# Small-matmul bursts of a recurrent mixer: one burst for the scores of a pair and one for the outputs of a step, with a wider spacing in the planner

## The chip, the cores and the metric

The kernel runs on one core of one Trainium2 chip. The metric is the device time of one execution in microseconds (us), lower is better. The engines are TensorE (PE in the profile, with its weight loads as PEld), VectorE (DVE), ScalarE (ACT), GpSimd (POOL) and SyncE (SP), which issues the transfers.

## The reference

A gated linear recurrence over 768 positions for 4 batches and 8 heads of 48, and two feed-forward layers on its 3072 rows:

```python
# attention: B, H, S, D = 4, 8, 768, 48
for t in range(S):
    cur = einsum('bhd,bhe->bhde', u * kt, vt)
    y[:, :, t] = einsum('bhd,bhde->bhe', rt, state + cur)
    state = wt[:, :, :, None] * state + einsum('bhd,bhe->bhde', kt, vt)
x = y.transpose(0, 2, 1, 3).reshape(3072, 384)
x = (sigmoid(x @ w_gate) * (x @ w_val)) @ moe_w_out     # 384 -> 1536 -> 384
h = x @ w_in                                            # 384 -> 2048
out = (h * tanh(softplus(h))) @ moe2_w_out              # 2048 -> 384
```

## The kernel before

The sequence is cut into 24 steps of 32 positions (`step(j)`), and two steps make a pair (`NP` = 12 pairs, numbered from 0). For a pair, `fine(p)` builds the products inside blocks of 8 positions on POOL and DVE (tiles `pt` and `blk`, sums in `A`), and `coarse(p)` turns what it needs (tiles `RD`, `KD`, `WD`) and computes the scores between blocks on TensorE (tile `lp`, two PSUM banks, L644). Eight tasks `merge` on ACT or DVE, three copies each, bring the scores from PSUM into the tile `X` (L665): four for the first step of the pair (bank `lp..0`), four for the second. Right behind the scores, one more product rescales 24 of the 56 columns of `RD` (L624, shape 128x768).

A step then has three pieces on TensorE. `rows_out` makes its outputs from `X` and `v` and from the state `s` and `RD` (tile `yp`, two PSUM banks, L742); a split into two half-precision parts follows on ACT and DVE (tile `xs`), and transposes send it to `xt`, the operand of the feed-forward layer. `outer` makes the update of the state (tile `kp`, L841), which DVE adds (`s`, L852). All three are bursts of small float32 matmuls with 32 or 64 rows and 48 columns; the tile program issues 64 of them for the scores of a pair, and the trace records two per matmul.

The feed-forward matmuls are the dense work: `gate` (tile `gv`, L901) and `out1` (tile `o`, L969), in groups of nine 128x128 by 128x256 matmuls. A pair has 24 groups of `gv` and, from the second on, 12 of `o`. While the dense groups of one pair run, the bursts of the next pair are put between them. The decoding of the weights (tiles `wgs`, `wvs`, `wos`, then `wis`, `wps`) is further work of ACT, DVE and POOL, at the beginning and after the last pair.

The three PSUM tiles `lp`, `yp` and `kp` share three banks in turn (`next_at`): the first bank of `kp` in the first step of a pair was the second of the scores, and its second bank was the first of `yp`.

The order of the work on each engine is not written by hand. Each piece is a task with a guessed cost and with the tiles that it reads and writes; `Plan.run` works out how late each may begin, then walks through time and gives each engine the task that is due earliest among those that are ready. A task may name two engines with a cost for each; the one that is free first takes it. Tasks marked `burst` are held back while another task is ready and the last burst ended less than `SPACE` ago:

```python
tired, late, rank, t = min(
    (t.burst and now < rested, t.late, t.rank, t) ...
if t.burst:
    rested = t.end + SPACE
```

Before, scores and outputs are each two tasks of cost `BURST` with the same operands and banks: half of the 8 (or 4) columns each.

Of the kernel before, what the change touches and what calls it, by code (L numbers as in the profile page):

```python
# [7 lines left out]
F32 = mybir.dt.float32  # L8
# [7 lines left out]
B, H, S, D = 4, 8, 768, 48  # L16
# [7 lines left out]
RC = 56  # L24
# [19 lines left out]
SHARED = (0,)  # L44
WHOLE = range(1, 12, 2)
COLD = 1.9
BURST = 0.58
PARTS = ((), (0,), (1,), (2, 3))
SPACE = 1.9
SWEEPS = 1  # L50
ENGS = ("pool", "dve")
W1HI = {"act": 0.83}
# [12 lines left out]
class Plan:  # L65
# [30 lines left out]
    def run(self):  # L96
# [35 lines left out]
        while len(order) < len(self.tasks):  # L132
# [14 lines left out]
            if t.burst:  # L147
                rested = t.end + SPACE
            if e != "none":
# [11 lines left out]
def mixer_moe_kernel(  # L161
# [30 lines left out]
    pp = sa.enter_context(tc.tile_pool(name="pp", bufs=1, space=PS, side="right"))  # L192
# [13 lines left out]
    def attn(eng, cost, fn, reads=(), writes=(), lat=SEM, burst=False):  # L206
        add(eng, cost, fn, [*reads, "attention"], writes, lat, burst)
# [217 lines left out]
    lps = {}  # L425
    late = {}
    yps = {}
# [8 lines left out]
    def next_at():  # L436
        nat[0] += 1
        return ("at", nat[0] % 3)
# [144 lines left out]
    def coarse(p, cells):  # L583

        R, K, W = (("blk", p % 2, i) for i in range(3))
        RD, KD, WD = ("RD", p % 2), "KD", ("WD", p % 2)
        X = [[("X", p % 2, e, n) for n in range(4)] for e in range(2)]
        banks = [next_at() for _ in range(2)]
# [39 lines left out]
                op=ALU.mult,  # L628
            )

        def scores(part):
            if not part:
                for e in range(2):
                    lps[p, e] = pp.tile(
                        [128, 8, RC - 8], F32, tag=f"at{banks[e][1]}", name=f"lp{p}_{e}"
                    )
            for i in range(4 * part, 4 * part + 4):
                for e in range(2):
                    for q in range(2):
                        for g in range(2):  # L640
                            o = 64 * (g ^ e) + 32 * q
                            x = HG * e + 8 * q + i
                            gs = slice(64 * g, 64 * g + 64)
                            nc.tensor.matmul(  # L644
                                lps[p, e][o : o + 32, i],
                                kd[p][gs, x],
                                rd[p][gs, x, 8:],
                                start=True,
                                stop=True,
                            )  # L650
# [21 lines left out]
        attn(both, 0, lambda e: scaled(e, 5, 6, 1, 2), [WD], [(*RD, 2)])  # L672
        attn({"dve": 0.6, "pool": 1.05}, 0, lambda e: scaled(e, 2, 4, 2, 1), [WD, (*RD, 2)], [(*RD, 1)])
        parts = [(*RD, n) for n in range(3)]
        for half in range(2):
            attn("pe", BURST, lambda _, n=half: scores(n), [*parts, KD], banks, burst=True)
        attn("dve", 1.9, flip_a, [*cells], X[0] + X[1])
        for e in range(2):
            for n in range(4):
# [40 lines left out]
    def step(j):  # L720
        p, e = divmod(j, 2)
        V = ("v", j % 3)
        X = [("X", p % 2, e, n) for n in range(4)]
        RD = [("RD", p % 2, n) for n in range(2)]
        S, nxt = ([("s", i % 2, x) for x in range(2)] for i in (j, j + 1))
        ybanks = [next_at() for _ in range(2)]

        def rows_out(part):
            if not part:
                for t in range(2):  # L730
                    yps[j, t] = pp.tile(
                        [128, 512], F32, tag=f"at{ybanks[t][1]}", name=f"yp{j}_{t}"
                    )
            for h in range(2 * part, 2 * part + 2):
                for n in range(2 if j else 1):
                    for t in range(2):
                        for b in range(B):
                            g = b // 2 ^ t
                            gs = slice(64 * g, 64 * g + 64)
                            i = b % 2 * H + 4 * t + h  # L740
                            x = HG * e + i
                            nc.tensor.matmul(  # L742
                                yps[j, t][32 * b : 32 * b + 32, h * D : h * D + D],
                                (rd if n else xp)[p][gs, x, :C],
                                (ss if n else vs)[j][gs, i, :],
                                start=(n == 0),
                                stop=(n == 1 or j == 0),
                            )
# [28 lines left out]
                    out=xt[p][:, i, :, 128 * e : 128 * e + 128], in_=xss[j][:, i]  # L777
                )

        for part in range(2):  # L780
            attn(
                "pe",
                BURST * (COLD if j < 4 else 1.0),
                lambda _, part=part: rows_out(part),
                [*X, *RD, V, *S],
                ybanks,
                burst=True,
            )
        xs = [("xs", j % 2, t) for t in range(2)]
        attn("none", 0, lambda _: new_xs(), [], [(*xs[t], i) for t in range(2) for i in range(2)])  # L790
        for t in range(2):
# [40 lines left out]
        kbanks = [next_at() for _ in range(2)]  # L832
# [31 lines left out]
                )  # L864
        cold = COLD if j < 4 else 1.0
        parts = [("KK", p % 2, g, q, h) for g in range(2) for q in range(2) for h in range(2)]
        attn("pe", 1.08 * cold, outer, [*parts, V], kbanks, burst=True)
        for hf in range(2):
            attn("dve", 0.48, lambda _, hf=hf: join(hf), [kbanks[hf]], [nxt[hf]])
        if j + 3 < NJ:  # L870
# [411 lines left out]
    for i in range(6):  # L1282
        cs = slice(256 * i, 256 * i + 256)
        for name, dst, w in (("wg", wgs, wg), ("wv", wvs, wv)):
            if count in WHOLE:
                load_raw((name, i), lambda: dp, in_cols(w, cs), (KC, 256), count % 3)
                part = lambda dst=dst, cs=cs: dst[:, :, :, cs]
# [11 lines left out]
    def tail1(p):  # L1299
        coarse(p, cells[p])  # L1300
        keys(p)
        step(2 * p)
# [134 lines left out]
```

## Time and profile before

| | us |
|---|---|
| time, median of three runs | 953.5 (953.48 to 955.08) |
| the profiled execution: its own time | 953.2 |
| its span, first to last instruction | 951.1 |
| PE busy | 887.4 (93%) |
| DVE busy | 653.6 (69%) |
| ACT busy | 484.7 (51%) |
| POOL busy | 478.5 (50%) |
| matmuls of `lp`, `yp`, `kp` in the trace | 1536, 3008, 1472 |

The profile is of one execution. A row of the timeline joins equal instructions that follow each other, with the start of the first and the time until the end of the last; ends of matmuls are modelled, so the start of the next row says more about the pace than the end does. What stands in brackets is idle time of the engine ahead of the row and what ended it. [...]

### The profile page before, as it was taken

How to read it: one execution, taken by the hardware profiler on the slowest of the kernel's cores; microseconds unless marked ns; L12 is line 12 of the kernel's file. 1: busy time of each engine (PE TensorE's matmuls, PEld its weight loads, DVE VectorE, ACT ScalarE, POOL GpSimd, SP SyncE). 2: the span in 40 equal slices, each digit the busy share in tenths (PEclk: the TensorE clock that was granted, in tenths of full speed). 3: DMA queues.
4: the chain of work that ended last, by engine and by line, in shares of the span. 5: the costliest groups of instructions: out<-in, count | busy, mean ns of one | idle time of the engine just before them, and what ended most of it. 6: DMA issues, size and time to landing. Idle time of an engine off the chain costs nothing.

```text
span 951.1 us, 29379 instructions
## 1 busy us (share of the span) xinstructions
PE 887.4 (93%) x12808; PEld 707.6 (74%) x12808; DVE 653.6 (69%) x1073; ACT 484.7 (51%) x1086; POOL 478.5 (50%) x528
## 2 busy tenths in 40 slices
PE   0478799999999999999999999999999999999998
PEld 0366478888888888888888886567677676776788
DVE  7999975666775867686678888785565655655541
ACT  2668854333435253433336777675565655556540
POOL 8999922636364546446364265553343434434330
PEclk9988799999999999999999999999999999999999
DMA  9456732222222223222222660010200102000000
GB/s 311 128 167 199 247 104 77 59 74 73 69 58 68 67 65 97 50 77 60 58 57 79 195 207 12 12 40 1 68 1 10 59 2 67 1 18 18 1 34 34
DMA packets 56464, 71.89 MB, mean 76 GB/s; under 512 B 20752, under 2 KB 37648, under 8 KB 56208
## 3 DMA queue, kind: packets, MB, share of 16 engines
q1 hardware_dynamic: 56336, 70.03, 24.9%
q8 instruction: 100, 1.64, 0.7%
q14 instruction: 28, 0.23, 0.1%
HBM read 56.64 MB, written 9.44 MB: 69 GB/s over the span
## 4 chain that ended last, share of the span: by engine, by line
PE 79%; DVE 8%; ACT 5%; POOL 4%; DMA 2%; issue 2%; SPq 0%; ACTq 0%; DVEq 0%; POOLq 0%
PE gv L901 23%; PE h L1079 20%; PE o L1194 17%; PE o L969 12%; ACT X L665 3%; PE yp L742 3%; PE kp L841 2%; DVE X L665 2%; PE lp L644 2%; POOL blk L487 1%; DMA raw_wp<-wo 1%; DVE A L507 1%; POOL sum_wp L333 1%; POOL pt L487 1%; DVE wps L333 1%
## 5 line engine op out<-in xcount | busy, mean ns | idle before, releaser
L1079 PE MATMUL h<-x,wis 128*128 128x512 f16 x864 | 199.9, 379 | 0.0
L487 POOL TENSOR_TENSOR blk<-blk 128x384 f32<-128x384 f32 (+3 forms) x139 | 124.0, 908 | 103.4 <-DMA blk<-rkw 72.0
L901 PE MATMUL gv<-xt,wvs 128*128 128x256 f16 x1296 | 169.1, 277 | 4.7 <-POOL wvs L307 3.7
L901 PE MATMUL gv<-xt,wgs 128*128 128x256 f16 x1296 | 167.2, 275 | 4.8 <-ACT sig L912 1.9
L969 PE MATMUL o<-gt,wos 128*128 128x256 f16 x1296 | 166.4, 274 | 3.7 <-POOL wos L307 2.0
L1113 POOL TENSOR_TENSOR sum<-e 128x256 f32<-128x256 f32 x96 | 71.4, 744 | 183.4 <-ACT e L1090 183.3
L1079 PEld LDWEIGHTS <-wis 128*128 128x128 f16 x864 | 83.5, 98 | 82.9
L901 PEld LDWEIGHTS <-wvs 128*128 128x128 f16 x1296 | 126.2, 99 | 23.4 <-POOL wvs L307 4.3
L969 PEld LDWEIGHTS <-wos 128*128 128x128 f16 x1296 | 126.5, 98 | 22.4 <-POOL wos L307 2.2
L901 PEld LDWEIGHTS <-wgs 128*128 128x128 f16 x1296 | 123.3, 98 | 23.6 <-issue 2.7
L487 POOL TENSOR_TENSOR pt<-blk 128x384 f32<-128x384 f32 x93 | 106.5, 1168 | 44.1 <-DMA blk<-rkw 42.5
L1090 ACT ACTIVATE e<-h 128x512 f32<-128x512 f32 x96 | 57.2, 596 | 84.6 <-PE h L1079 83.7
L929 ACT CAST gt<-gv 128x512 f16<-128x512 f32 x72 | 42.0, 584 | 77.3 <-DVE gv L917 77.1
L665 ACT COPY X<-lp 24x64 f32<-24x64 f32 x180 | 46.1, 256 | 54.8 <-DVE X L665 26.0
L1194 PE MATMUL o<-wps,gt 128*128 128x192 f16 x612 | 74.0, 246 | 0.0
L917 DVE SCALAR_TENSOR_TENSOR gv<-gv,sig 128x512 f32<-128x512 f32 x72 | 50.8, 706 | 33.2 <-ACT sig L912 16.7
L912 ACT ACTIVATE sig<-gv 128x512 f32<-128x512 f32 x72 | 43.2, 599 | 52.8 <-PE gv L901 52.5
L932 DVE TENSOR_TENSOR gt<-gv,gt 128x512 f16<-128x512 f32 x72 | 49.4, 686 | 29.1 <-ACT gt L929 28.6
L1132 DVE SCALAR_TENSOR_TENSOR gt<-e,gt 128x256 f16<-128x256 f32 x41 | 27.5, 683 | 49.6 <-ACT gt L1127 49.6
L1194 PE MATMUL o<-wps,wgs 128*128 128x192 f16 x498 | 59.4, 246 | 0.0
L1194 PE MATMUL o<-wps,wos 128*128 128x192 f16 x456 | 57.1, 246 | 0.0
L1194 PEld LDWEIGHTS <-gt 128*128 128x128 f16 x612 | 52.9, 98 | 3.3
(107 smaller groups left out, 1470.0 us busy)
## 6 DMA issues: line engine op xcount, KB each, us to landing
v<-vt SPq DMA_DIRECT2D x96, 96.0 KB, 3.0
blk<-rkw SPq DMA_DIRECT2D x22, 384.0 KB, 3.4
raw_wi<-wi SPq DMA_DIRECT2D x8, 768.0 KB, 5.9
raw_wp<-wo SPq DMA_DIRECT2D x8, 768.0 KB, 6.2
blk<-rkw SPq DMA_DIRECT2D x11, 512.0 KB, 3.7
raw_wg<-wg SPq DMA_DIRECT2D x6, 768.0 KB, 6.1
raw_wv<-wv SPq DMA_DIRECT2D x6, 768.0 KB, 7.2
raw_wo<-wo SPq DMA_DIRECT2D x6, 768.0 KB, 5.3
```

Of the source, the lines that this page charges most:

```text
L487: engines[e].tensor_tensor(out=pv, in0=a, in1=b, op=ALU.mult)
L665: put(out=xp[p][o : o + t, xs, t:], in_=lps[p, e][i : i + t, :, c : c + C - t])
L901: nc.tensor.matmul(gps[p, i, o][:, h], w[:, a, kc, fs], xt[p][:, c, kc, :], start=(n == 0), stop=(n == 3 * KC - 1),)
L912: nc.scalar.activation(out=sgs[p, i], in_=gps[p, i, 0], func=AF.Sigmoid, scale=1.0 / (SW * SX))
L917: nc.vector.scalar_tensor_tensor(out=gps[p, i, 1], in0=gps[p, i, 1], scalar=SG / (SW * SX), in1=sgs.pop((p, i)), op0=ALU.mult, op1=ALU.mult,)
L929: nc.scalar.copy(out=gt[p][:, 0, 2 * i : 2 * i + 2], in_=gps[p, i, 1])
L932: nc.vector.tensor_tensor(out=gt[p][:, 1, 2 * i : 2 * i + 2], in0=gps[p, i, 1], in1=gt[p][:, 0, 2 * i : 2 * i + 2], op=ALU.subtract,)
L969: nc.tensor.matmul(ops[p, c][:, :NT], wos[:, a, f, cs], gt[p][:, g, f, :], start=(f == 0 and n == 0), stop=(f == NF1 - 1 and n == 2),)
L1079: nc.tensor.matmul(hps[r, f], w2["wi"][:, a, kc, fs], x2[r][:, c, kc, :], start=(n == 0), stop=(n == 3 * KC - 1),)
L1090: nc.scalar.activation(out=es[r, f], in_=hps[r, f], func=AF.Mish, scale=ih)
L1113: engines[e].tensor_tensor(out=sums[0][:, n - 1], in0=a(), in1=b(), op=op)
L1194: nc.tensor.matmul(ops2[h, first], home(slots[r, i, name])[:, c, tsl], w2["wp"][:, a, w, i, :], start=(new and n == 0), stop=(n == 3 * NF2 ...
```

## The change

Scores of a pair become one task, outputs of a step one task, each with all its matmuls in one burst. The planner's numbers change with it: `BURST` from 0.58 to 1.42, `SPACE` from 1.9 to 3.0, the cost of `outer` from 1.08 to 1.17. These numbers only set the order; no instruction of the arithmetic is added or taken away.

```diff
-BURST = 0.58
+BURST = 1.42
-SPACE = 1.9
+SPACE = 3.0
...
-        def scores(part):
-            if not part:
-                for e in range(2):
-                    lps[p, e] = pp.tile(
-                        [128, 8, RC - 8], F32, tag=f"at{banks[e][1]}", name=f"lp{p}_{e}"
-                    )
-            for i in range(4 * part, 4 * part + 4):
+        def scores(_):
+            for e in range(2):
+                lps[p, e] = pp.tile(
+                    [128, 8, RC - 8], F32, tag=f"at{banks[e][1]}", name=f"lp{p}_{e}"
+                )
+            for i in range(8):
...
-        for half in range(2):
-            attn("pe", BURST, lambda _, n=half: scores(n), [*parts, KD], banks, burst=True)
+        attn("pe", BURST, scores, [*parts, KD], banks, burst=True)
...
-        def rows_out(part):
...
-            for h in range(2 * part, 2 * part + 2):
+        def rows_out(_):
...
+            for h in range(4):
...
-        for part in range(2):
-            attn(
-                "pe",
-                BURST * (COLD if j < 4 else 1.0),
-                lambda _, part=part: rows_out(part),
-                [*X, *RD, V, *S],
-                ybanks,
-                burst=True,
-            )
+        cold = COLD if j < 4 else 1.0
+        attn("pe", BURST * cold, rows_out, [*X, *RD, V, *S], ybanks, burst=True)
...
-        attn("pe", 1.08 * cold, outer, [*parts, V], kbanks, burst=True)
+        attn("pe", 1.17 * cold, outer, [*parts, V], kbanks, burst=True)
```

What the planner makes of it is shown at three places of pair 8, whose scores are computed while the dense groups of pair 7 run. In names such as `gv7_2_0` the numbers are the pair, the gate and its half (0 is `wgs`, 1 is `wvs`); `o16_1` is `out1` of pair 6, second column block; `lp8_0` and `lp8_1` are the two banks of the scores; `yp16` is step 16, the first of the pair. Line numbers of the changed kernel are lower by 1 to 12.

On TensorE, before, from the end of the first half of the scores to the first outputs:

```order
L644 MATMUL lp8_0_6137<-RD8_5890,KD8_5952 32x48 x4
L644 MATMUL lp8_1_6138<-RD8_5890,KD8_5952 32x48 x4
L901 LDWEIGHTS wgs_88
L901 MATMUL gv7_2_0_6172<-xt7_5641,wgs_88 128x256
...
L901 MATMUL gv7_2_1_6186<-xt7_5641,wvs_89 128x256
L644 MATMUL lp8_0_6137<-RD8_5890,KD8_5952 32x48 x4
...
L901 MATMUL gv7_2_0_6172<-xt7_5641,wgs_88 128x256
...
L969 MATMUL o16_1_6261<-gt6_5346,wos_90 128x256
L742 MATMUL yp16_0_6277<-v16_5118,X8_5872 32x48 x4
L742 MATMUL yp16_1_6278<-v16_5118,X8_5872 32x48 x4
```

Two groups of `gv` stand between the halves of the scores, and three dense groups between the second half and the outputs. The same place now:

```order
L643 MATMUL lp8_0_6136<-RD8_5897,KD8_5952 32x48 x4
L643 MATMUL lp8_1_6137<-RD8_5897,KD8_5952 32x48 x4
L889 LDWEIGHTS wgs_88
L889 MATMUL gv7_2_0_6209<-xt7_5606,wgs_88 128x256
...
L889 MATMUL gv7_2_1_6229<-xt7_5606,wvs_89 128x256
L737 MATMUL yp16_0_6275<-v16_5135,X8_5836 32x48 x4
L737 MATMUL yp16_1_6276<-v16_5135,X8_5836 32x48 x4
```

The scores are one row of bursts, and four dense groups (two of each half of gate 2) stand between them and the outputs. Counted from score to score, a pair from 3 to 10 had before, as groups between bursts: 2 (to the second half), 3, 2, 2, 2, 2, 2, and 21 after the last; now it has 4, 4, 4, 4 and 20. It is 36 groups in both.

On DVE, before, from the end of a gate to the next gate, the rescaling of `RD` and three merges:

```order
L932 TENSOR_TENSOR gt7_6099<-gv7_1_1_6089,gt7_6099 128x512
L216 SCALAR_TENSOR_TENSOR xo_6182<-o16_0_6038,xo_6182 128x256
L624 TENSOR_TENSOR RD8_5890<-RD8_5890,WD8_5914 128x32x24
L665 COPY X8_5872<-lp8_0_6137 24x8x8
L665 COPY X8_5872<-lp8_0_6137 16x8x16
L665 COPY X8_5872<-lp8_0_6137 8x8x24
L665 COPY X8_5872<-lp8_1_6138 24x8x8
...
L917 SCALAR_TENSOR_TENSOR gv7_2_1_6186<-gv7_2_1_6186,sig_6327 128x512
```

Now there are four merges, two of them for the first step, and no rescaling:

```order
L920 TENSOR_TENSOR gt7_6099<-gv7_1_1_6089,gt7_6099 128x512
L664 COPY X8_5836<-lp8_0_6136 24x8x8
L664 COPY X8_5836<-lp8_0_6136 16x8x16
L664 COPY X8_5836<-lp8_0_6136 8x8x24
L664 COPY X8_5836<-lp8_0_6136 24x8x8
...
L664 COPY X8_5836<-lp8_1_6137 24x8x8
...
L905 SCALAR_TENSOR_TENSOR gv7_2_1_6229<-gv7_2_1_6229,sig_6273 128x512
```

The merges that DVE gained are those that ACT lost (it had three of the first step and two of the second, and has two and two). The rescaling stands on POOL now, behind the first products of the next pair and ahead of the updates of its `blk`:

```order
L487 TENSOR_TENSOR pt_6076<-blk9_5274 128x768
L487 TENSOR_TENSOR pt_6101<-blk9_5274 128x384
L624 TENSOR_TENSOR RD8_5897<-RD8_5897,WD8_5916 128x32x24
L487 TENSOR_TENSOR blk9_5274<-blk9_5274 128x16x24 x2
L487 TENSOR_TENSOR pt_6374<-blk9_5274 128x8x48 x2
```

It moved so in pairs 4 to 10; in pairs 3 and 11 it stays on DVE.

## Rows read from the trace of the kernel before

**Rows 1.** Profile page, TensorE's granted clock in 40 equal slices, in tenths.
```profile
PEclk9988799999999999999999999999999999999999
```

**Rows 2.** Stretch table: length, busy time of each engine, granted clock, DMA share, GB/s.
```profile
167.00:519.00 352.00, 349.79 (x6833) 302.38 (x6833) 250.96 (x397) 139.03 (x343) 179.51 (x192) 1.00 0.25 66
```

**Rows 3.** Timeline, TensorE, scores and steps of pair 8: start, duration, instructions, idle.
```profile
384.08 1.15 PE L969 MATMUL o<-gt,wos 128*128 128x256 f16 x9
385.16 0.81 PE L644 MATMUL lp<-RD,KD 64*32 64x48 f32 x64
385.89 1.16 PE L901 MATMUL gv<-xt,wgs 128*128 128x256 f16 x9
...
387.96 0.80 PE L644 MATMUL lp<-RD,KD 64*32 64x48 f32 x64
...
391.75 0.28 PE L742 MATMUL yp<-v,X 64*32 64x48 f32 x6
392.31 0.26 PE L742 MATMUL yp<-v,X 64*32 64x48 f32 x5 [0.28 <-ACT X L665]
...
393.00 1.16 PE L901 MATMUL gv<-xt,wgs 128*128 128x256 f16 x9
...
397.88 1.36 PE L841 MATMUL kp<-v,KK 32*64 32x48 f32 x64
399.17 1.16 PE L901 MATMUL gv<-xt,wvs 128*128 128x256 f16 x9
...
406.85 1.15 PE L841 MATMUL kp<-v,KK 32*64 32x48 f32 x64
407.93 1.16 PE L901 MATMUL gv<-xt,wvs 128*128 128x256 f16 x9
...
428.66 0.81 PE L644 MATMUL lp<-RD,KD 64*32 64x48 f32 x64
```

**Rows 4.** Timeline, TensorE, a whole step's outputs in one burst (step 4).
```profile
125.85 0.31 PE L742 MATMUL yp<-v,X 64*32 64x48 f32 x15
...
126.90 0.33 PE L742 MATMUL yp<-s,RD 64*32 64x48 f32 x13
129.15 1.14 PE L901 MATMUL gv<-xt,wgs 128*128 128x256 f16 x9 [1.92 <-ACT sig L912]
```

**Rows 5.** Timeline, ACT and DVE behind the scores of pair 8.
```profile
388.74 1.68 ACT L665 COPY X<-lp 24x64 f32<-24x64 f32 x6 [2.79 <-PE lp L644]
391.42 0.84 ACT L665 COPY X<-lp 24x64 f32<-24x64 f32 x3 [1.00 <-DVE X L665]
...
390.45 1.89 DVE L665 COPY X<-lp 24x64 f32<-24x64 f32 x6 [0.66 <-ACT X L665]
...
397.70 0.61 DVE L216 SCALAR_TENSOR_TENSOR xs<-yp,xs 128x192 f16<-128x192 f32 x2
```

**Rows 6.** Timeline, POOL around the scores of pair 8.
```profile
390.67 1.96 POOL L487 TENSOR_TENSOR blk<-blk 128x384 f32<-128x384 f32 x2 [9.46 <-DMA blk<-rkw]
```

**Rows 7.** Groups by line and shape, POOL: busy us, mean ns, idle before.
```profile
L624 POOL TENSOR_TENSOR RD<-RD,WD 128x768 f32<-128x768 f32 x2 | 3.0, 1478 | 1.0 <-PE lp L644 1.0
```

**Rows 8.** Waits of TensorE from 60 to 145 us: total, times, longest.
```profile
PE gv L901 <- POOL wvs L307: 3.7, 2, 2.8
...
PE o L969 <- POOL wos L307: 2.0, 1, 2.0
```

**Rows 9.** Timeline, POOL, ahead of the last `wvs` of the first stage.
```profile
89.91 5.32 POOL L487 TENSOR_TENSOR pt<-blk 128x384 f32<-128x384 f32 x4
```

**Rows 10.** Stretch table, around two whole bursts and a stretch at reduced clock.
```profile
82.30:83.90 1.60, 1.46 (x130) 1.24 (x128) 1.60 (x3) 1.35 (x3) 0.00 (x0) 1.00 1.03 224
...
125.80:129.20 3.40, 1.48 (x131) 1.39 (x130) 1.94 (x6) 2.30 (x9) 0.00 (x0) 1.00 0.02 5
...
100.00:104.00 4.00, 3.46 (x17) 2.41 (x18) 2.43 (x3) 3.49 (x5) 4.00 (x4) 0.57 0.35 100
```

**Rows 11.** Waits of TensorE from 516 to 584 us.
```profile
PE gv L901 <- DVE gt L932: 0.8, 1, 0.8
```

More of the change, by code (lines that the diff above doesn't have):

```diff
@@ L726, in step @@
         ybanks = [next_at() for _ in range(2)]
-        def rows_out(part):
[L729 to L732, printed above, removed]
-                    )
-            for h in range(2 * part, 2 * part + 2):
+        def rows_out(_):
+            for t in range(2):
+                yps[j, t] = pp.tile([128, 512], F32, tag=f"at{ybanks[t][1]}", name=f"yp{j}_{t}")
+            for h in range(4):
                 for n in range(2 if j else 1):
@@ L778, in send @@
                 )
-        for part in range(2):
-            attn(
-                "pe",
-                BURST * (COLD if j < 4 else 1.0),
-                lambda _, part=part: rows_out(part),
-                [*X, *RD, V, *S],
-                ybanks,
-                burst=True,
-            )
+        cold = COLD if j < 4 else 1.0
+        attn("pe", BURST * cold, rows_out, [*X, *RD, V, *S], ybanks, burst=True)
         xs = [("xs", j % 2, t) for t in range(2)]
```

## Prediction

> **What bounds the kernel now.** I read the clock row first, then the stretch table, then TensorE's timeline of one pair. The clock dips only in the first eighth of the span [rows 1], so there are two regimes. Up to about 110 us the engines wait for each other and for decoded weights. From there on TensorE is the bound: from 167 to 519 us it is busy 349.79 of 352 us at full clock, while DVE, the next, has 250.96 [rows 2]. In that regime a microsecond less on TensorE is a microsecond less in the end, as long as nobody else becomes late. Pairs 3 to 10 repeat each other; I take pair 8, from its scores at 385.16 to the next at 428.66 [rows 3]: 43.50 us.
>
> What fills it: from the group at 407.93 to the scores at 428.66 there are 21 dense groups, 20.73 us less 0.10 of entry, so 0.983 us a group, and 36 of them are 35.4 us. The other 8.1 us are eight bursts. The reader should see three kinds of them.
>
> A half burst has 64 recorded matmuls. The group at 384.08 would hand over at 385.06; the burst starts at 385.16 and the next group at 385.89 [rows 3], so it costs 0.83 us. Six of the eight are halves (two of scores, four of outputs), all of this pace.
>
> The first outputs are held up: five matmuls follow at 392.31 after a wait for a merge on ACT, and the next group comes at 393.00, 1.25 after the burst's start at 391.75 instead of 0.73 [rows 3]. This burst costs 1.34: 0.51 of waiting.
>
> The state update costs 1.17 in the second step (406.85 to 407.93, with 0.09 of entry) but 1.38 in the first (397.88 to 399.17) [rows 3]. Its second bank was the first of the outputs, and DVE's split of these runs from 397.70 [rows 5], two of 0.3 us: 0.21 of waiting.
>
> **The price of one burst in place of two.** The trace has whole bursts of outputs already, where the planner put two halves side by side. The one at 125.85 has 128 matmuls; its last row begins at 126.90 and ends, as modelled, at 127.23 [rows 4]. The group behind it came only at 129.15, held up by ACT, so its exit has to be taken from the halves: there the next group starts 0.08 before the modelled end (385.97 against 385.89) [rows 3]. So 127.15, which is 1.30 after the start, and with the entry of 0.10 a whole burst costs 1.40, two halves 1.66. The merge saves 0.26. It is not 0.83, because the second 64 matmuls still take 0.57; what goes is one entry, one exit and the pause in the middle.
>
> [...]
>
> **Pairs 3 to 10.** Three merges each: -0.78.
>
> The wait for the first outputs. Before, the merges could start only behind the second half (ACT at 388.74, 0.78 after 387.96 [rows 3, 5]), and three groups later the outputs were due. Now they start behind the one burst: at its modelled end, 1.38 after its start [rows 4] less 0.02, so at 1.36. They pass the tile X to and fro: ACT waits for DVE and DVE for ACT [rows 5]. With two on each engine the four of the first step take 0.84, 0.94, 0.84 and 0.94 (0.84 for three copies on ACT, 1.89 for six on DVE [rows 5]) and some 0.03 for each hand-over: ready at about 5.0. The outputs are due when the burst (1.30) and four groups (3.93) are through, with the entry at 5.3. So the wait of 0.51 goes, with 0.3 to spare; the bounds are 0 and 0.51, and I take 0, which is nearer to 0.3 of slack than to none. What is late next is the rescaling of RD, now on POOL. POOL stands idle there for 9.46 us [rows 6], and the same shape took it 1.48 [rows 7]: ready at about 2.9. If that idle time were gone, outputs would wait for POOL's queue.
>
> The wait of the state update: the outputs begin at 5.3 and are through at 6.65; the update is due four groups later, at 10.7. Before it was due two groups behind the second half. ACT and DVE finish all eight merges at about 7.8 (a second chain of four as long, beginning on ACT when its second merge is done, at 4.0), one gate's product follows, and the two splits of 0.3 end near 9.8. So -0.21, with 0.9 to spare. The gates that ACT and DVE handle later for it need their banks two gates on, some 10 us later, and cost nothing.
>
> The sum: 35.4 + 3 x 1.40 + 2 x 1.17 = 41.95, with 0.05 for groups that start 0.01 late behind bursts 42.0. Against 43.5: -1.5 a pair, and **-12.0** for eight.
>
> **Pair 2.** Scores and one step are merged (step 4 was whole): -0.5. Its waits I leave: TensorE waited 1.92 for a sigmoid behind the outputs [rows 4], and now the update of the state stands where DVE has nine more rows ahead of the split.
>
> **Pair 11 and the decoding behind it.** Three merges, -0.8. TensorE waits 1.6 us in that stretch, 0.8 of it for DVE [rows 11], which has weights to decode there; the merges start 1.4 earlier relative to the first score matmul, so some of it goes. I take -0.5 out of 0 to -1.6: **-1.3** in all. Behind 583 us TensorE has no wait, and nothing there is touched.
>
> **The first stage.** The new costs shuffle decoding and the first pairs. TensorE waited 3.7 us for the last values of `wvs` and 2.0 for `wos` on POOL [rows 8]. POOL now does the last `wvs` ahead of two of the four products at 89.91 (5.32 for the four [rows 9]), some 2.7 us earlier, and a block of `wos` went to DVE. But what these groups gain, pair 2 can wait away, since DVE has more to do than before. I take **-1.2**, between -5.7 (both waits gone) and +3.
>
> The sum: -12.0 - 0.5 - 1.3 - 1.2 = -15.0. Against the profiled execution's 953.2 that is 938.2, and with the median 0.3 above it **938.5 us**.
>
> **The rivals.**
>
> The waits stay. For it: the slack of 0.3 is less than one merge, and one more task ahead of the merges on ACT or DVE eats it. Against it: ACT stood idle for 2.79 us ahead of its merges [rows 5]. If all eight pairs keep 0.51 and 0.21: +5.8, 944.3.
>
> A whole burst has a slower exit. Both whole bursts of the trace are followed by a wait, so no row shows the exit by itself. If the merge saved 0.03 instead of 0.26: 29 x 0.23 = 6.7 more, 945.2.
>
> The first stage loses. If order and decoding there cost 10 us instead of giving 1.2, it would be 949.7.
>
> Slower: the clock falls behind the longer bursts. For 1.4 us the array does only small matmuls, and stretches of those with waits among them are where the clock was low early on. [...] Against it: around both whole bursts that the trace has at full pace (128 matmuls each, within 82.30 to 83.90 and 125.80 to 129.20) the clock is 1.00, even with 1.92 us of idleness behind the second [rows 4, 10]. [...]
>
> It doesn't do what it says: bursts are merged, but what TensorE saves appears as a wait for merges, splits and decoding, pair by pair. Then 953.5. Against it stands DVE's idle time of 100 us in the long stretch [rows 2].
>
> **How the numbers follow.** The forecast 0.62; waits stay 0.14; slow exit 0.07; first stage loses 0.07; clock 0.04; no change 0.03; better than all of it 0.03. The range: below, the first stage at -5.7 (4.5 more) and the tail's waits all gone (1.1 more), 932.9; above, the slow exit at 945.2 and half a microsecond of the tail's gain not made: 933.0 to 946.0, which holds the first three cases, 0.83. A measurement of this kernel can tell about 0.2% from no change; faster by more than that 0.93, within it 0.03, slower 0.04.
>
> **What would show it.** Right: 42.0 us from scores to scores in pairs 4 to 10; rows of 64 matmuls doubled to 128, with the next group 1.30 behind the start; no wait for X ahead of outputs; both state updates at 1.17. Wrong: a wait of TensorE for ACT or DVE copies of X or for POOL's RD; a granted clock below 1.00 behind 145 us; the scores of pair 3 later than 167 us by more than 2.

## The result, and the profile after

The changed kernel takes 940.74 us, the median of four runs (939.37 to 941.42); the kernel before, on the same chip, 953.49 (952.21 to 955.08). The ratio is 0.9864 with an interval of 0.9845 to 0.9883. The prediction was 938.5 and its range 933.0 to 946.0. The profiled execution after took 939.37, its span is 937.7, so it is 1.4 faster than the median, while the profiled one of before lies 0.3 below its own. Medians and ratios here are of runs in the fast state; one run of the kernel before (2294.55) and one of shift64 (1811.88) were in a slow one.

The total fits, but not its parts. From the first scores of one pair to those of a later one:

| | before | after | difference | predicted |
|---|---|---|---|---|
| start to the scores of pair 3 | 167.6 | 160.8 | -6.8 | -1.7 |
| pairs 3 to 10 | 348.05 | 340.48 | -7.6 | -12.0 |
| scores of pair 11 to the end of the span | 435.4 | 436.4 | +1.0 | -1.3 |
| span | 951.1 | 937.7 | -13.4 | -15.0 |

The eight pairs last 41.98, 44.21, 41.98, 43.63, 41.98, 42.74, 41.98 and 41.98 us. Five of them are what the sum had said (42.0); three are not. TensorE's timeline of pair 9, one of the five, answers to [rows 3, 4] (start, duration, instructions):

```profile
417.33 1.38 PE L643 MATMUL lp<-RD,KD 64*32 64x48 f32 x128
418.64 1.16 PE L889 MATMUL gv<-xt,wgs 128*128 128x256 f16 x9
...
422.67 0.31 PE L737 MATMUL yp<-v,X 64*32 64x48 f32 x15
...
423.99 1.16 PE L957 MATMUL o<-gt,wos 128*128 128x256 f16 x9
...
428.02 1.15 PE L829 MATMUL kp<-v,KK 32*64 32x48 f32 x64
429.10 1.16 PE L889 MATMUL gv<-xt,wvs 128*128 128x256 f16 x9
...
438.48 1.15 PE L829 MATMUL kp<-v,KK 32*64 32x48 f32 x64
439.56 1.16 PE L957 MATMUL o<-gt,wos 128*128 128x256 f16 x9
...
459.31 0.90 PE L643 MATMUL lp<-RD,KD 64*32 64x48 f32 x75
```

The 128 matmuls of the scores are one row, and the next group starts 1.31 behind the first of them. With the entry of 0.10 the burst costs 1.41, as predicted (1.40); so do the outputs, 422.67 to 423.99, which no merge holds up. Both updates cost 1.17 (428.02 to 429.10 and 438.48 to 439.56, with 0.09 of entry).

ACT and DVE behind the same scores, as in [rows 5], and POOL, as in [rows 6]:

```profile
418.68 0.83 ACT L664 COPY X<-lp 24x64 f32<-24x64 f32 x3 [0.38 <-PE lp L643]
419.54 0.92 DVE L664 COPY X<-lp 24x64 f32<-24x64 f32 x3 [0.52 <-ACT X L664]
420.50 1.70 ACT L664 COPY X<-lp 24x64 f32<-24x64 f32 x6 [0.99 <-DVE X L664]
421.36 1.94 DVE L664 COPY X<-lp 24x64 f32<-24x64 f32 x6 [0.90 <-ACT X L664]
...
427.12 0.61 DVE L216 SCALAR_TENSOR_TENSOR xs<-yp,xs 128x192 f16<-128x192 f32 x2
...
418.82 1.48 POOL L624 TENSOR_TENSOR RD<-RD,WD 128x768 f32<-128x768 f32 x1 [5.17 <-PE lp L643]
```

The chain of copies runs to and fro as the prediction laid it out. Its fourth member is done at about 422.3, 5.0 after 417.33; the outputs start at 422.67. The update at 428.02 finds the splits done at 427.73. The slack is 0.3 at both places (0.3 and 0.9 were predicted). POOL's rescaling is done at 420.30.

The clock row of the page and the stretch of eight pairs answer to [rows 1, 2]. The columns of the stretch are length, busy time of PE, PEld, DVE, ACT and POOL, granted clock (as a share of full speed), DMA share, GB/s:

```profile
PEclk9989899999999999999999999999999999999999
...
160.80:501.30 340.50, 336.40 (x6691) 296.78 (x6690) 252.44 (x406) 132.02 (x321) 188.47 (x197) 1.00 0.25 66
```

From the sixth slice on the clock row shows 9, and in the stretch of eight pairs the granted clock is 1.00. But TensorE stands idle for 4.1 of 340.5 us, where before it was 2.2 of 352. Its waits in that stretch and from 495 to 585 us, as in [rows 11], are (total, times, longest):

```profile
PE yp L737 <- issue: 2.0, 2, 1.4
PE o L957 <- DVE xo L216: 1.6, 1, 1.6
PE gv L889 <- ACT xs L213: 0.5, 1, 0.5
...
PE gv L889 <- issue: 2.0, 1, 2.0
PE yp L737 <- issue: 0.9, 1, 0.9
PE gv L889 <- DVE gt L920: 0.7, 1, 0.7
```

No wait for X is left and, as the next section shows of the 0.5 put down to ACT's `xs`, none for the splits; in their place stand a wait for DVE's `xo` (the split of an `out1` sum, in pair 4) and one that is put down to no engine at all, "issue". The experiments are about these two and about the three stretches of the table.

### The profile page after: what moved, and what is told of

The parts are those of the page before. It is cut to its first block, busy times and chain, and to the rows that moved or that the text cites. A ratio compares the mean times of both kernels' runs of the same rounds, so it can differ in the third digit from the quotient of the medians.

```text
span 937.7 us, 29380 instructions
## 1 busy us (share of the span) xinstructions
PE 874.2 (93%) x12808; PEld 703.9 (75%) x12808; DVE 661.3 (71%) x1094; ACT 479.1 (51%) x1065; POOL 487.7 (52%) x528
## 3 DMA queue, kind: packets, MB, share of 16 engines
q8 instruction: 100, 1.64, 0.8%
## 4 chain that ended last, share of the span: by engine, by line
PE 78%; DVE 11%; ACT 5%; DMA 3%; issue 2%; POOL 1%; SPq 0%; ACTq 0%; DVEq 0%; POOLq 0%
PE gv L889 22%; PE h L1067 20%; PE o L1182 18%; PE o L957 13%; PE yp L737 2%; PE kp L829 2%; DVE X L664 1%; ACT X L664 1%; PE lp L643 1%; DMA raw_wp<-wo 1%; ACT KK L705 1%; DVE A L507 1%; DVE KD L605 1%; DVE WD L616 1%; DVE pt L487 1%
## 5 line engine op out<-in xcount | busy, mean ns | idle before, releaser
L889 PE MATMUL gv<-xt,wvs 128*128 128x256 f16 x1296 | 166.3, 274 | 1.3 <-DVE gt L920 0.7
L889 PEld LDWEIGHTS <-wgs 128*128 128x128 f16 x1296 | 126.5, 99 | 28.9 <-ACT X L664 6.0
L624 POOL TENSOR_TENSOR RD<-RD,WD 128x256 f32<-128x256 f32 (+2 forms) x32 | 33.6, 1050 | 63.2 <-PE lp L643 32.9
L920 DVE TENSOR_TENSOR gt<-gv,gt 128x512 f16<-128x512 f32 x72 | 49.3, 684 | 16.6 <-ACT gt L917 15.6
L664 ACT COPY X<-lp 24x64 f32<-24x64 f32 x159 | 40.7, 256 | 34.1 <-DVE X L664 25.9
```

Of the source, the lines that this page charges most:

```text
L664: put(out=xp[p][o : o + t, xs, t:], in_=lps[p, e][i : i + t, :, c : c + C - t])
L889: nc.tensor.matmul(gps[p, i, o][:, h], w[:, a, kc, fs], xt[p][:, c, kc, :], start=(n == 0), stop=(n == 3 * KC - 1),)
L920: nc.vector.tensor_tensor(out=gt[p][:, 1, 2 * i : 2 * i + 2], in0=gps[p, i, 1], in1=gt[p][:, 0, 2 * i : 2 * i + 2], op=ALU.subtract,)
```

## What "issue" is

Pair 6 has such a pause inside the outputs, with matmuls of the same operands (`s` and `RD`) on both sides of it:

```profile
297.08 0.28 PE L737 MATMUL yp<-s,RD 64*32 64x48 f32 x4 [1.41 <-issue]
```

The page shows a queue that the prediction had not looked at:

```profile
q8 instruction: 100, 1.64, 0.8%
```

A hundred packets of 16,384 bytes; 1.64 MB over TensorE's 25,616 instructions (12,808 matmuls and as many weight loads) is 64 bytes each, so one packet carries 256 instructions, or 128 matmuls: an estimate from the page. long_scores, one of the experiments below, bears it out: with 3,328 weight loads and matmuls more its page has 113 packets, 13 more, and 3,328 by 13 is 256. A whole burst of scores or outputs of the changed kernel uses up one such block in 1.18 us (first matmul to last, 417.33 to 418.51 in pair 9); nine matmuls of a dense group take 0.98 us, a block 13.9. Blocks can be followed through the trace. For some of them: when the block before came into use, when this transfer began and ended, when its first matmul ran, how long that is behind the transfer's end, and the distance to the matmul before it:

```
kernel       block  previous  transfer        first     behind  distance
             no.    in use    began   ended   matmul    its end to last
after         33     263.35   264.20  265.40  268.49     3.09    0.01
after         44     338.46   339.27  340.68  343.58     2.90    0.01
after         26     220.23   219.70  220.70  222.13     1.43    0.73
after         37     293.91   294.40  295.64  297.08     1.44    1.61
after         50     377.99   379.38  380.36  381.75     1.39    0.79
after         69     501.89   505.64  506.58  507.93     1.34    1.11
after         72     518.26   521.36  522.37  523.60     1.23    2.29
late_loads    69     504.38   505.21  506.12  509.30     3.18    0.01
late_loads    72     519.71   519.87  521.03  522.86     1.83    0.11
```

Of 62 blocks between 137 and 566 us of the changed kernel none was used less than 1.23 us behind the end of its transfer; five came into use 1.23 to 1.44 behind it, and these five have a pause ahead of them, 0.5 to 2.0 us of it idle. The next in rank, 1.65 and more, have none. In this kernel, where dense work lies ahead, a transfer begins up to 1.8 us before the block ahead of it is in use, and borders 1.93 us apart do without a pause (block 62); where a burst lies ahead, it begins 0.3 to 1.5 behind, and with 0.9 to 1.5 of transfer and some 1.4 until use two borders need 2.6 to 4.4 us between them, an estimate from these rows (3.17 and 3.76 at blocks 37 and 50, with their pauses). A whole burst goes through a block in 1.18, so a burst that begins shortly behind a border, or a few groups behind it, reaches the next too early. The wait of 0.5 that the list puts down to ACT's `xs` is block 26. The same counting puts the wait in pair 4 elsewhere: that one is not at a border.

The place in the stream settles it. TensorE's instructions can be numbered (weight loads, matmuls and its semaphore instructions). All 50 idle times of 0.3 us and more that the fourteen traces put down to issue between 137 and 566 us then end at instruction 193 or 194 of 256. One of them is in the kernel before: 0.6 us at 143.9 us.

In the changed kernel a block of dense work alone, 13.9 us of it, has no such pause behind it. The five pauses follow blocks that hold a burst, in which TensorE goes through 256 instructions in as little as 1.18 us; block 37 came 3.17 behind the one before it.

## The experiments

Twelve kernels take the result apart. The kernel before, run beside them, took 952.67 to 952.99 us.

**The spacing without the merge, and the merge without the spacing.** First before with `SPACE` 3.0 and `outer` 1.17 (halves kept), then after with `SPACE` 1.9.

```diff
-SPACE = 1.9
+SPACE = 3.0
-        attn("pe", 1.08 * cold, outer, ...
+        attn("pe", 1.17 * cold, outer, ...
```

> The kernel before with only the planner's numbers changed: SPACE 3.0 and the update's cost 1.17, bursts still in halves. Four dense groups then stand between all bursts of a pair. If merging and waiting are two separate gains, each half still costs 0.83 and the update 1.17, but the waits of 0.51 and 0.21 are gone: 42.8 us a pair, 8 x 0.72 = 5.8 us below the kernel before in pairs 3 to 10, about 947 us. If the spacing makes the whole gain: 42.0 a pair, 941. If the merging makes all of it: 43.5 a pair, 953.

> The changed kernel with SPACE back at 1.9: whole bursts, with three dense groups from scores to outputs and two from outputs to the state update. If the copies of the scores and the split of the outputs end last, they are ready 5.0 us and about 9.8 us after the scores begin, so the outputs (due at 4.35) wait 0.7 and the update (then due at 8.4) waits 1.3: 44.0 a pair, about 955 us. If only the number of bursts counts: 42.0 a pair, 941.

Measured: 954.63 us (ratio 1.0011, 0.999 to 1.0031) and 952.29 (1.0000, 0.9987 to 1.0013). Neither part gives anything alone. TensorE's waits in pairs 3 to 10, of the first and of the second:

```profile
PE gv L901 <- DMA xt<-xs: 3.1, 4, 1.5
PE gv L901 <- DMA blk<-rkw: 2.6, 1, 2.6
...
PE yp L737 <- DVE X L664: 2.8, 7, 0.4
PE gv L889 <- issue: 2.1, 2, 1.1
PE kp L829 <- DVE xs L216: 1.6, 3, 0.6
PE yp L737 <- issue: 1.3, 2, 0.9
```

With four groups between them, eight bursts reach far into a pair: the second update follows its outputs after one group or none, 11 groups are left behind it where 21 were before, and the dense work of the next pair waits for its operand `xt` (3.1 us; the 2.6 put down to a load of `blk`, which `gv` doesn't read, is probably the same wait). Five whole bursts with two or three groups between them wait for merges and splits. The first expectation missed by 7.6 us, since it had looked for the waits that go and not at where the bursts end; the second had the right mechanism and was 2.7 too slow.

**One half of the merge alone**, both with the new spacing.

> One part of the merge: scores in one burst, outputs in halves, spacing 3.0, update 1.17. A pair has six bursts four groups apart (4, 4, 4, 4, 4 and 12 behind the last), so unlike the eight of halves_spaced they fit into the pair. If the spacing removes the waits wherever the bursts fit, and a merge saves its 0.26: 36 groups 35.4, scores 1.40, four halves 3.32, two updates 2.34, 42.46 a pair, pairs 3 to 10 in 339.7 us, with fewer stalls by the supply of instructions than the changed kernel has, since only the scores are a block of 256 instructions on end: 340 to 341, as much as the 340.5 of the changed kernel; time 941 to 944. If both merges are needed, the pairs stay at 43.5 and the time at 952.

> The other part: outputs in one burst, scores in halves. Gaps of 4, 4, 4, 4, 4 and 16 groups. Without stalls 36 groups 35.4, two halves 1.66, two whole outputs 2.80, two updates 2.34, 42.20 a pair, 337.6 for eight; with 2 to 4 us of supply stalls at the whole outputs 339.6 to 341.6. Time 941 to 944. If both merges are needed, 43.5 a pair and 952.

Measured: 948.73 us (0.9955, 0.9935 to 0.9975) and 941.71 (0.9879, 0.9859 to 0.9898). With the outputs whole and the scores in halves the eight pairs take 337.95 us, 42.24 each, and TensorE is never idle:

```profile
164.60:502.60 338.00, 338.00 (x6696) 296.65 (x6699) 246.99 (x407) 130.29 (x318) 189.87 (x199) 1.00 0.25 66
```

That is the 42.20 of the expectation without its stalls: no pause falls into these pairs. Why not is not shown. Borders lie as near as 1.7 us there too, and two blocks came into use only 1.34 and 1.37 us behind their transfers, as close as in the changed kernel's pauses, so it may be luck of the places. Its tail has two pauses (3.1 and 0.6 us). This half of the change is as good as all of it: it gives 0.26 a pair away and has none of the pauses in pairs 3 to 10. With the scores whole and the outputs in halves, every other pair takes 42.51 (expected 42.46) and the rest 43.5 to 44.2, where the first half of the outputs waits for merges (a fifth wait of 0.4 is for ACT's). With the scores of pair 3 at 165.8 besides, the 941 to 944 expected were missed by some 5:

```profile
PE yp L749 <- DVE X L669: 2.7, 4, 0.7
```

**Where the instruction blocks end.** After, with 32 or 64 matmuls of 32 columns ahead of the first `out1`, which it overwrites: the places of all borders move by so many matmuls.

```diff
+            if p == 0 and c == 0 and part == 0:
+                for _ in range(32):
+                    nc.tensor.matmul(
+                        ops[p, c][:, :32],
...
```

> The changed kernel with 32 small extra matmuls at the first output group of pair 0, where TensorE waits for decoded weights (their results are overwritten); everything behind is the same, but 32 matmuls later in TensorE's stream of instructions. In the changed kernel outputs of pairs 4, 6 and 8 stall by 1.65, 1.65 and 0.76 us. If the supply of instructions makes these stalls (16 KB, 128 matmuls with their weight loads, in one fetch), they depend on where a burst lies in the block of 128: the three are free now (104, 112 and 120 instead of 72, 80 and 88), while scores that come to lie at 76 and 84 (pairs 6 and 8) may stall. If a copy or a split on another engine makes them, the same three stalls stay.

> As the last one, with 64 extra matmuls. If the supply of instructions makes the stalls, pairs 4, 6 and 8 are free and outputs that come to lie at 76 to 92 in their block stall: the first of pairs 5 and 7, and the second steps of pairs 3 and 5, by 0.5 to 1.7 us each. If another engine makes them, outputs of pairs 4, 6 and 8 stall as in the changed kernel, by 1.65, 1.65 and 0.76.

Measured: 942.28 us (0.9889, 0.9854 to 0.9924) and 941.76 (0.9882, 0.9861 to 0.9903). The pauses of pairs 6 and 8 are gone in both; there are others, with 32 in pair 9 (0.9 us) and with 64 in pairs 3 (0.3), 5 (0.8) and 7 (1.63, again in outputs). The wait of pair 4 is still there, 1.64 us, both times for `xo`. So pauses put down to issue go with the place in the stream, and pair 4's doesn't. Which bursts would be hit was forecast poorly. Of four places that I had named for 64, pair 7 came in full and pair 5 in part; the second steps of pairs 3 and 5 didn't. With 32 the scores of pairs 6 and 8 did not stall, and pair 9 had not been named.

**Longer bursts.** After, with the scores of pairs 5 and 7 issued four times and those of pair 9 eight times.

```diff
-            for i in range(8):
+            for i in [*range(8)] * LONG.get(p, 1):
```

> The changed kernel with the scores' matmuls of pairs 5 and 7 issued four times over and those of pair 9 eight times (the repeats write the same values again), so 3, 3 and 7 times 256 more instructions, which is 3, 3 and 7 whole blocks of the instruction transfers. If TensorE's own pace sets a burst of small matmuls, the repeats go on at 1.18 us for each 128 recorded matmuls: bursts of 4.96 (pairs 5 and 7) and 9.70 us (pair 9), time 940.7 + 15.4 = 956. If the supply limits them, a block costs the transfer (1.0 to 1.5) and 1.2 to 1.5 behind its end, 2.4 in all: bursts of 7 to 8.6 and 16 to 18.5 us, with pauses near multiples of 128 recorded matmuls, time 965 to 972. If transfers run ahead and only follow each other, 1.2 to 1.5 per block: 5 to 6 and 10 to 12 us.

Measured: 996.3 us in a single run, and bursts of 11.9, 12.4 and 27.6 us, longer than every case had it. TensorE's timeline in pair 9, and its stretch (columns as above):

```profile
445.89 2.05 PE L644 MATMUL lp<-RD,KD 64*32 64x48 f32 x205
450.11 1.71 PE L644 MATMUL lp<-RD,KD 64*32 64x48 f32 x128 [2.17 <-issue]
454.15 1.77 PE L644 MATMUL lp<-RD,KD 64*32 64x48 f32 x128 [2.32 <-issue]
457.89 1.77 PE L644 MATMUL lp<-RD,KD 64*32 64x48 f32 x128 [1.97 <-issue]
...
445.00:474.00 29.00, 14.92 (x1036) 13.22 (x1035) 2.27 (x4) 1.34 (x5) 0.41 (x1) 0.59 0.09 23
```

After every 128 matmuls TensorE stops for 1.7 to 2.3 us, with nothing else to wait for and the DMA engines at 9%. Seven more blocks cost 26.2 us, 3.74 each (27.62 less 1.40, by 7), where TensorE's own pace is 1.18. The supply is the limit, and a slower one than the 2.4 us I had expected: in pair 9 the transfer starts only 0.9 to 1.2 us behind the first matmul of the block before, takes 1.0 to 1.4, and is used 1.2 to 1.6 behind its end. In these stretches of pauses the granted clock falls too, 0.59 on average, which lengthens the rows of 128 to about 1.5 from start to start of first and last. That is the smaller part: the first block border in the scores of pair 5 still has the full clock and a pause of 1.9 us.

**Pair 4's wait.** After, with the split of one sum made urgent in the planner; TensorE's order stays the same row for row.

```diff
+        for t in plan.tasks[-2:]:
+            t.ahead = AHEAD * (p == 2 and c == 0)
```

> The changed kernel, with one column block of pair 2's out1 given 10 us of urgency in the planner, so that DVE splits its sum (xo) ahead of the merges of pair 4's scores and not behind them; TensorE's order stays the same row for row. If the 1.65 us of pair 4 (outputs at 208.14, next group of out1 at 211.10) is DVE's order, the stall goes: that burst 1.40, pair 4 at 42.0 to 42.6 instead of 44.21, span 936.1 and time 939.1. If it is the supply of instructions, which the position in TensorE's stream decides, it stays at 1.6 since the stream is the same, and the time is 940.7. The waits at the outputs of pairs 6 and 8 should stay within 0.5 of their 1.65 and 0.76, at the same places in the stream.

Measured: 940.01 us (0.9864, 0.9848 to 0.9880). DVE behind the scores of pair 4, in after and then in this kernel:

```profile
206.83 1.94 DVE L664 COPY X<-lp 24x64 f32<-24x64 f32 x6 [0.90 <-ACT X L664]
209.66 0.93 DVE L664 COPY X<-lp 24x64 f32<-24x64 f32 x3 [0.89 <-ACT X L664]
210.62 0.42 DVE L216 SCALAR_TENSOR_TENSOR xo<-o,xo 128x256 f16<-128x256 f32 x1
...
205.09 0.41 DVE L220 SCALAR_TENSOR_TENSOR xo<-o,xo 128x256 f16<-128x256 f32 x1
206.05 0.92 DVE L668 COPY X<-lp 24x64 f32<-24x64 f32 x3 [0.55 <-ACT X L668]
```

The wait of 1.6 us is gone, so it was DVE's order: in after the split stands behind four merges, and the next `out1` needs its bank. Yet the pair gains 0.70 (44.21 to 43.51) and not 1.65. Being early, TensorE runs into the supply, which it had reached in time before: 0.47 behind the next group and 1.06 instead of 0.59 at the outputs of the second step. A stall that is taken away makes room for the next in line.

**The two gains apart.** Before with only pairs 0 to 2 planned the new way (below), and with only pairs 3 to 11 (the conditions turned round).

```diff
+SCORES = lambda p: p < 3
+OUTPUTS = lambda j: j < 6
+SPACE = lambda p: 3.0 if p < 3 else 1.9
+UPDATE = lambda p: 1.17 if p < 3 else 1.08
```

> Pairs 0 to 2 are planned as after the change (whole bursts, spacing 3.0, update 1.17), pairs 3 to 11 as before it (halves, spacing 1.9, update 1.08); TensorE's order is that of the kernel before from its row 1,111 of 14,522 on. My theory is that the change has two gains that add: one in the first stage, where the scores of pair 3 came at 160.8 us instead of 167.6, and one in pairs 3 to 10 (340.5 instead of 348.05 us). Then this kernel has the first alone: scores of pair 3 at 160.8 to 162, pairs 3 to 10 in 348 us, time 946.3. The rival is that the early gain exists only together with the later pairs' planning, or that TensorE takes it back as a wait behind pair 3: then 951 to 953.5.

> The reverse: pairs 0 to 2 as before the change, pairs 3 to 11 as after it. The theory that the two gains add gives scores of pair 3 at 167 to 168 us, pairs 3 to 10 in 340 to 341 us with a stall in the first outputs of pair 4, and 946.5 in all. If instead the whole gain belongs to pairs 3 to 11 as my prediction had it, 941 to 942; if the later gain needs the early order, 951 or more. The stalls of TensorE with idle time put down to issue should move to other pairs, since the rows of TensorE ahead of them are others in time but the same in number.

Measured: 948.13 us (0.9958, 0.9945 to 0.9971) and 946.64 (0.9931, 0.9909 to 0.9953), 4.8 and 6.3 less than before (946.3 and 946.5 were expected). Both gains are real, and they add to 11.1 of the 12.75. The early one is the less steady: the scores of pair 3 came at 164.5 in early_only (pairs 3 to 10 then took 348.04, as before), and in the five kernels with the early order of after at 160.8 to 163.7, of which the profiled execution of the result is the earliest. In late_only the pairs take 343.4, since pair 10 has a pause of 0.7 more and one of 1.8 us in pair 6 had a sequel, here with its stretch:

```profile
302.96 0.28 PE L749 MATMUL yp<-s,RD 64*32 64x48 f32 x4 [1.79 <-issue]
303.17 1.81 PE L976 MATMUL o<-gt,wos 128*128 128x256 f16 x9
304.77 2.13 PE L908 MATMUL gv<-xt,wgs 128*128 128x256 f16 x9
...
303.40:306.80 3.40, 3.40 (x19) 2.47 (x17) 2.50 (x5) 0.79 (x2) 3.32 (x4) 0.52 0.17 34
```

The granted clock is 0.52 for 3.4 us, and two groups take nearly twice their time: 1.65 us more. Two other kernels have such a spell in the tail: whole_outputs with the pause of 3.1 us (0.51 from 515.9 to 519.3) and shift32 behind two of 1.3 and 1.7 us (0.50 from 512.6 to 516.0).

**The tail.** After, with the loads of `wi` and `wp` held until the last piece of the recurrence is issued.

```diff
+        add("none", 0, open_b, [], ["attention", "open"])
...
-            load_raw(("wi", i), lambda: dp, in_cols(wi, cs), (KC, 256), i % 3)
+            load_raw(("wi", i), lambda: dp, in_cols(wi, cs), (KC, 256), i % 3, ["open"])
...
-        add("none", 0, open_b, [], ["attention", "open"])
...
-            reads = [] if slot < 3 else ["open"]
+            reads = ["open"]
```

> The changed kernel with the loads of the last two weight matrices (wi, wp) held until the last piece of the recurrence is issued. In the changed kernel they move 66% of the DMA engines' time between 495 and 530 us, and there the blocks of TensorE's instructions start 2.8 to 3.7 us behind the use of the block before them, elsewhere 0.3 to 1.5. If that is where the tail's stalls come from, the one in the outputs at 506.6 (1.04) and the one at 521.3 (2.0) go and the transfer of instructions starts within 1.5 us of the block before until about 525 us: 3 us less in the tail, 937 to 938, and less still if the first stage gains from five loads and their decoding that move out of it. The rival: the decoding of wis is late then, and TensorE waits for it ahead of the last layers (first matmuls of h at 583): 5 us or more lost, 945 to 955.

Measured: 951.88 us (0.9996, 0.9985 to 1.0007). Both theories were right, and the rival weighs more. The stretch from 495 to 530 us in before, after and here:

```profile
495.00:530.00 35.00, 34.41 (x541) 29.80 (x539) 27.19 (x41) 20.83 (x45) 11.96 (x11) 1.00 0.22 66
...
495.00:530.00 35.00, 32.08 (x692) 28.05 (x690) 29.70 (x46) 24.48 (x49) 9.32 (x5) 1.00 0.67 179
...
495.00:530.00 35.00, 35.00 (x722) 30.94 (x720) 13.96 (x31) 15.14 (x37) 1.49 (x1) 1.00 0.19 52
```

With the DMA engines at 0.67 TensorE stands idle for 2.9 us, with 0.19 not at all, and the blocks of instructions begin within 1.0 us of the one before (the table above) instead of 3.1 to 3.8. Then the decoding comes due all at once, and TensorE waits for DVE:

```profile
PE gv L889 <- DVE gt L920: 5.7, 2, 4.7
```

From the scores of pair 11 to the end it is 447.6 us instead of 436.4.

The fixed window hides one thing: pair 11 comes 14 us later in the kernel before, and its bursts meet the loads as well. In the 25 us from its scores on the DMA engines are at 0.69 in before and at 0.75 in after, and in before a transfer began as late as 4.4 us behind the use of the block ahead of it. Yet with halves TensorE lost only 0.3 us to issue there. So the loss goes with both, loads and whole bursts; mixed, with halves there (below), lost 0.7.

**A mixture.** Pairs 0 to 2 as after, pairs 3 to 10 with whole outputs and halves of scores, pair 11 in halves with the old spacing.

```diff
+SCORES = lambda p: p < 3
+OUTPUTS = lambda j: j < 22
+SPACE = lambda p: 3.0 if p < 11 else 1.9
+UPDATE = lambda p: 1.17
```

> A version put together from what the runs showed: pairs 0 to 2 as in the changed kernel (scores at 160.8 to 163.7 for pair 3 in its runs), pairs 3 to 10 with outputs whole and scores in halves, four groups apart (338.0 us without a stall in whole_outputs; on TensorE, DVE and ACT the order of these pairs is the same here), pair 11 in halves with the spacing of before, so that no block of 256 instructions runs on end while the last weights are loaded (whole_outputs lost 3.5 and 0.8 us there, the kernel before 0.5). Expected: scores of pair 3 at 162, pairs 3 to 10 in 338, from the scores of pair 11 to the end 435.4 (before) to 436.4 (after): span 936, time 937.5 (936 to 939), which beats the 940.7 of the changed kernel by 0.3%. Rival: the place of the weight loads decides the tail, whatever the bursts are: another stall of 3 us there, 940 to 941. Rival: the three stretches don't add, 943 or more.

Measured: 940.85 us (0.9872, 0.9852 to 0.9892), no better than the changed kernel. Pairs 3 to 10 take 338.07 as expected, but the scores of pair 3 come at 165.1 instead of 162, and the tail takes 437.0. The three stretches are planned together, and what one gains here another loses. No version that beats 940.7 by more than the runs scatter was found.

## Why the prediction was right, and where it wasn't

**The price of a burst: right.** 1.40 predicted, 1.41 by the rows of pair 9.

**The waits that go: right.** X is ready 0.3 ahead of the outputs, the updates cost 1.17 both times, POOL's rescaling is hidden. Five of eight pairs are 41.98. What the prediction did not see is that this needs both parts: with halves the wide spacing leaves too little of a pair behind the last burst, with whole bursts the narrow one brings the waits back.

**Pairs 3 to 10: the step that failed is "the sum".** It holds for a pair without new waits, and 4.6 us of new ones came in three pairs: 1.65 in pair 4 from DVE's order behind the new merges, and 0.59, 1.65 and 0.76 from the supply of instructions. The first was there to be found in the order of the changed kernel. For the second the prediction asked which engine or transfer would be late next, and the transfer of TensorE's own instructions wasn't on its list, although the page before has the queue, with the same 100 packets. So the term that was put at nothing without a reason is this supply: 3.0 us in the pairs, and 2.9 in the tail.

**The first stage and pair 2: a term that was mis-sized.** -1.7 was taken and -6.8 came in the profiled run, just outside of the first stage's bounds with pair 2's 0.5. By the medians of early_only it is nearer to -4.8. The waits of [rows 8] for POOL's `wvs` fell from 3.7 to 0.7 and those for POOL's `wos` from 2.0 to 0.2, as the prediction had it for its lower bound, but DVE and ACT now have `wos` late (2.7 and 1.9), and a new wait of 7.3 for DVE stands at 60 to 65 us:

```profile
PE gv L889 <- DVE gt L920: 7.3, 2, 5.9
PE o L957 <- DVE wos L307: 2.7, 2, 2.5
PE o L957 <- ACT wos L304: 1.9, 1, 1.9
...
PE gv L889 <- POOL wvs L307: 0.7, 1, 0.7
```

All rows of that list come to 16.6 us, those of before to 19.1, so 2.5 us are waits. Counted by matmuls, the 900th comes 3.1 us earlier than before, the 1,200th (at 97 us) 6.3 and the 2,100th (at 156 us) 6.8.

The clock is another part: TensorE's granted clock was 0.5 for 17.1 us instead of 23.9 in before, which is 3.4 us of work. But that part comes and goes. long_scores, planned like the changed kernel up to pair 3, spent 23.9 us at 0.5, as long as before, and its scores of pair 3 came at 163.4, 4.2 earlier than before. late_only, with pairs 0 to 2 planned as before, spent 17.1 there, and they came at 166.3, only 1.3 earlier. So some 4 us are the new order, and the clock has 1 to 3 that another execution need not show. The stretches that hold these spells in after, and two of before:

```profile
60.00:70.00 10.00, 4.21 (x24) 3.09 (x25) 8.31 (x16) 8.37 (x23) 9.92 (x8) 0.66 0.44 133
70.00:80.00 10.00, 8.60 (x231) 6.32 (x228) 9.55 (x19) 8.43 (x17) 9.92 (x12) 0.83 0.42 137
100.00:107.00 7.00, 4.26 (x21) 2.69 (x21) 7.00 (x6) 6.04 (x9) 6.92 (x6) 0.51 0.70 217
...
66.00:81.00 15.00, 10.22 (x223) 7.50 (x224) 12.80 (x25) 11.63 (x31) 14.92 (x17) 0.54 0.45 148
107.00:115.00 8.00, 5.99 (x32) 4.01 (x31) 7.71 (x7) 6.92 (x11) 7.12 (x6) 0.57 0.82 266
```

Which of the planner's numbers brought this about was not tried apart, and stays open.

**The tail: wrong in sign.** -1.3 was expected and +1.0 came. The waits for other engines fell as forecast, from 1.3 (0.8 for DVE's `gt` and 0.5 for a split) to 0.7. But the last weights are loaded while the bursts of pair 11 run, instruction blocks come late, and whole bursts pay for it with two pauses of 0.9 and 2.0 us, where halves paid 0.3. late_loads shows the loads' part: without them there is no pause.

**The rivals.** The waits for X and the splits did not stay, and there is no slow exit. A lower clock behind whole bursts was not seen in the changed kernel; behind or with pauses it was, in late_only (0.52), whole_outputs (0.51) and shift32 (0.50). The stretch of before at 0.57 in [rows 10] (100 to 104 us) was no case of small matmuls: it holds 17 matmuls of the dense groups, behind a wait of 2.8 us. So the total came out near the forecast by luck: 5.1 us more at the beginning covered 4.4 less in the pairs and 2.3 less in the tail.

## What to carry to other kernels

A burst of small matmuls had a price here that merging saved (1.41 us for a whole one, 0.83 for each half), but the longer burst also asked for instructions faster than they came: a block of 256 was used up in 1.18 us, and where bursts ran on end (long_scores) each block took 3.74. So count the instructions, and look at the instruction queue beside the engines when a wait is put down to nothing. Work that is spread wider must still fit ahead of the next consumer, so spacing and size of the pieces are one choice and are tried together. And a total that fits is no proof of its parts: compare stretch by stretch.

## What the runs showed of the hardware

In the scores of pair 9 of long_scores a block of 256 TensorE instructions came every 3.5 to 4.0 us (mean 3.74 for a block), while TensorE goes through one in the scores or outputs of the changed kernel in 1.18. No block was used within 1.23 us of the end of its transfer in the changed kernel, or within 1.19 in the kernel before. With weight loads on the DMA engines (0.67 of their time from 495 to 530 us) the transfers of the changed kernel began up to 3.8 us behind the use of the block before, otherwise, between 137 and 500 us and with one exception of 2.4, up to 1.5. Pauses of 1.7 to 2.3 us that follow each other (long_scores, 445 to 474 us) went with a granted clock of 0.59. A single one of 1.8 us (late_only), one of 3.1 (whole_outputs) and two of 1.3 and 1.7 (shift32) went with 0.50 to 0.52 for 3.4 us; others of 1.4 and 2.0 us in the changed kernel (at 297 and 523 us) left it at 1.00.
